# A new order for the first three chunks of a linear-attention and two-MoE kernel

## The chip, the cores and the metric

The program runs on one core of a Trainium2 chip. The metric is the device time in microseconds. Inputs and outputs are those of the reference, in float32.

## The reference, cut to what matters

```python
B, H, S, D = 4, 8, 768, 48
for t in range(S):                                   # linear attention with a decaying state
    cur = einsum('bhd,bhe->bhde', u * k_t, v_t)
    y_t = einsum('bhd,bhde->bhe', r_t, state + cur)
    state = w * state + einsum('bhd,bhe->bhde', k_t, v_t)
x = y.transpose(0, 2, 1, 3).reshape(3072, 384)
p = domain_probs / domain_probs.sum(-1)              # first MoE: 4 experts, all used, 1024 hidden
x = sum(p[:, e] * (relu(x @ w1[e]) @ w2[e]) for e in range(4))
# second MoE: 8 experts; each row goes to one expert by sorted gate logits, 384 rows each
out[rows of e] = relu(x[rows of e] @ v1[e]) @ v2[e]
```

## The kernel before, in words

The time axis is cut into 24 chunks of 128 positions, six to a batch element. A chunk's attention is done in closed form. Its transposed r and k (tile rkT, 512 KB) are multiplied by tables of powers of w (`mul`, L915). TensorE makes the scores (`scores`, L959), VectorE masks them (`am`, L965), and TensorE multiplies them with v and adds the part of the carried state S (`y_mm`, L983 and L987). The state for the next chunk comes from `state` (TensorE L1004, VectorE L1008, L1009 and L1011); it needs k times a table (`kn`, L929, on GpSimd). The diagonal term goes over GpSimd: `rk` (L921), `ru` (L925), then a sum on VectorE (`cc`, L940) and `cv` (L946). `x_add` (L994) joins both, and `tr` transposes x on TensorE (L1020) and stores it as an upper part by ScalarE (L1022) and a remainder by VectorE (L1023).

Every matrix of the MoE stages is held as two float32r parts, upper part and remainder, and a product is three matmuls: upper by upper, upper by remainder, remainder by upper (`up`, L1119, L1121, L1123; `down`, L1140, L1142, L1144). A weight of 384 KB comes into `raw` in pairs; ScalarE copies the upper part (L1058) and GpSimd or VectorE subtracts it (L1059), which is `split`.

The first MoE runs in 32 units of 384 rows by one expert. A unit is eight `up` blocks and three `down` groups. Its instruction stream has 48 ticks, one after every three matmuls, at which the Python program pops a step of a later chunk out of `queue` and puts it into the streams. Chunks 0, 1 and 2 are needed before the first unit, chunks 3, 4 and 5 before the second.

So there is a prologue. First come the tables of powers: `scan`, `inverse` and `mirror` for four pairs of heads, all on VectorE. Then a branch on a flag, and then chunks 0, 1 and 2 in an order written by hand, with bursts of empty matmuls (`warm`, L1284; also L703 and L724) between. All engines run their streams in the written order. Loads are issued by SyncE in the written order; a load waits there for its buffer.

Of the kernel before, what the change touches and what calls it, by code (L numbers as in the profile page):

```python
# [631 lines left out]
def rwkv_moe_moe(ctx, tc, A, out):  # L632
    nc = tc.nc
# [55 lines left out]
    with tc.tile_pool(name="psum0", bufs=1, space=bass.MemoryType.PSUM) as psum, tc.manual_schedule():  # L689
        v = nc.vector  # L690
        pb = psum.tile([128, 128], F32, name="pb")
        pf = psum.tile([1, 1], F32, name="pf")
        v.memset(busy, 0.0)
        v.memset(ones, 1.0)
        v.memset(zero, 0.0)
        v.memset(tp[:, 0, :, 64:65], 1.0)
        v.memset(tp[:, 1, :, 63:64], 1.0)
        v.memset(w128m, 0.0)
        make_identity(nc, ident)
        nc.gpsimd.iota(jp, pattern=[[1, 128]], base=0, channel_multiplier=-1)  # L700
# [20 lines left out]
        scan(0)  # L721
        v.tensor_scalar(flag, pf, 511.5, None, op0=OP.is_ge)
        for _ in range(36):
            nc.tensor.matmul(pb, busy.to_broadcast([128, 128]), busy.to_broadcast([128, 128]), start=True, stop=True)  # L724
        scan(1)
        inverse(0)
        scan(2)
        mirror(0)
        inverse(1)
        scan(3)  # L730
        mirror(1)
        inverse(2)
        inverse(3)
        mirror(2)
        mirror(3)
# [90 lines left out]
def main(ctx, tc, A, out, C, stepwise):  # L826
# [82 lines left out]
    def attn_steps(ck, detail=False):  # L909
# [6 lines left out]

        def rk():
# [23 lines left out]

        def cv():
# [3 lines left out]
            nc.gpsimd.tensor_tensor(r3, v3, st.pop((ck, "c")).to_broadcast([128, 8, 48]), op=OP.mult)  # L946

# [13 lines left out]
        def am(p0=0, p1=4):  # L961
            if p0 == 0:
                st[ck] = at.tile([128, 2, 4, 128], F32, name="am", bufs=1)
            for s in range(2):
# [11 lines left out]

        def y_mm():
            t, n = ld[ck]
            v = n[:, 384:768]
            y = psum.tile([128, D], F32, name="at", bufs=4)  # L980
            for p in range(4):
                if c:
                    nc.tensor.matmul(y[:, 96 * p:96 * p + 96], t[:, 0, p, :], S[ck - 1][:, p, :],  # L983
                                     start=True, stop=False)
                for s in range(2):
# [10 lines left out]

        def state():
            if c == 5:
                return
            t, n = ld[ck]  # L1000
            v = n[:, 384:768]
            p_ = psum.tile([128, 4, 96], F32, name="at", bufs=4)
            for p in range(4):
                nc.tensor.matmul(p_[:, p, :], n[:, 768 + 128 * p:896 + 128 * p], v[:, 96 * p:96 * p + 96],  # L1004
                                 start=True, stop=True)
            s = at.tile([128, 4, 96], F32, name="S", bufs=2)
            if c:
# [5 lines left out]

        def tr():
# [3 lines left out]
            p = psum.tile([128, 3, 128], F32, name="at", bufs=4)  # L1018
            for d in range(3):
                nc.tensor.transpose(p[:, d, :], x[:, 128 * d:128 * d + 128], ident)  # L1020
            cs = slice(128 * c, 128 * c + 128)
            nc.scalar.activation(XT[b][:, 0, :, cs], p, AF.Copy)  # L1022
            nc.vector.tensor_sub(XT[b][:, 1, :, cs], p, XT[b][:, 0, :, cs].bitcast(F32))  # L1023
            ld.pop(ck)

# [9 lines left out]
        if detail:  # L1035
            return dict(mul=mul, rk=rk, ru=ru, kn=kn, cc=cc, cv=cv, scores=scores, am=am, y=y_mm, x=x_add, state=state, tr=tr)
        return [lambda: (mul(nc.vector), pre()), pre2, nothing, att, nothing, yy, nothing, tr]
# [72 lines left out]
    def up(xT, c0, after1, before1, tick, tick1=lambda: None, place=None, H=None):  # L1110
        H = [] if H is None else H
        for f in range(FB):
            before1(f)
            p = psum.tile([128, D], F32, name="mm", bufs=4)
            w = W1[f]
            for k in range(3):
                ks = slice(128 * k, 128 * k + 128)
                xh, xl = xT[:, 0, k, c0:c0 + 384], xT[:, 1, k, c0:c0 + 384]
                nc.tensor.matmul(p, w[:, 0, ks], xh, start=(k == 0), stop=False)  # L1119
                tick1()  # L1120
                nc.tensor.matmul(p, w[:, 0, ks], xl, start=False, stop=False)  # L1121
                tick1()
                nc.tensor.matmul(p, w[:, 1, ks], xh, start=False, stop=(k == 2))  # L1123
                if k < 2:
                    tick()
# [103 lines left out]
    def tick():  # L1229
# [41 lines left out]
    else:  # L1271
        load_chunk(0)
        load_chunk(1)
        load_w(1, A["w1"], wl[0], 0)
        load_chunk(2)
        for q in range(1, 4):
            load_w(1, A["w1"], wl[0], q)
        consts_in()
        load_chunk(3)
        def warm(n):  # L1280
            p = psum.tile([128, 128], F32, name="mm", bufs=4)
            b = C["busy"].to_broadcast([128, 128])
            for _ in range(n):
                nc.tensor.matmul(p, b, b, start=True, stop=True)  # L1284

        def pkn_in():
            pt = psum.tile([128, 4, 128], F32, name="at", bufs=4)
            for p in range(4):
# [11 lines left out]
        a["mul"](nc.gpsimd, 0, 1)  # L1300
        a["mul"](nc.gpsimd, 1, 2)
        a["mul"](nc.vector, 2, 4)
        a["scores"](0, 1)
        warm(6)
        a["scores"](1, 2)
        pkn_in()
        a["am"](0, 2)
        a["scores"](2, 4)
        a["rk"]()
        a["ru"]()  # L1310
        a["am"](2, 4)
        a["kn"]()
        b["mul"](nc.vector)
        warm(8)
        a["cc"]()
        w128_in()
        b["rk"]()
        a["cv"]()
        a["y"]()
        a["state"]()  # L1320
        b["kn"]()
        b["scores"](0, 4)
        a["x"]()
# [6 lines left out]
        c["scores"](0, 4)  # L1330
        b["cc"]()
        b["cv"]()
        b["y"]()
        c["am"]()
        c["ru"]()
        split(1, 0, wl[0])
        b["x"]()
        c["cc"]()
        c["state"]()
        a["tr"]()  # L1340
        c["cv"]()
        split(1, 1, wl[0])
        split(1, 2, wl[0])
        split(1, 3, wl[0])
# [12 lines left out]
    nxt_chunk = [6]
    for ui, (i, blk) in enumerate(units):
# [353 lines left out]
```

## Time and profile before

| | us |
|---|---|
| median of 3 runs | 1229.07 (1228.4 to 1231.1) |
| profiled execution, its own time | 1224.69 |
| span of the profiled execution | 1222.9 |
| TensorE busy | 1199.3 (98%) |
| mean granted clock of TensorE | 0.988 of full |

The time of an execution is a little longer than the span from the first to the last instruction (here by 1.8 us). The granted clock is the share of full speed that TensorE was given: 1.00 is 2.4 GHz and 0.50 is 1.2 GHz. Busy time of an engine doesn't tell whether its clock was full. In the rows, PE is the matmul side of TensorE, PEld its weight load, DVE is VectorE, ACT ScalarE, POOL GpSimd and SPq the queue of SyncE, which issues the loads.

### The profile page before, as it was taken

To read this page: it belongs to the slowest core of one execution; us is meant where nothing else is said; L and a number is where in the kernel's file an instruction comes from. 1 tells how busy PE (TensorE), PEld (TensorE's weight loads), DVE (VectorE), ACT (ScalarE), POOL (GpSimd) and SP (SyncE) were. 2 spreads that over 40 slices of the span, in tenths; PEclk is the share of its full clock that TensorE was granted. 3 is DMA by queue.
4 is the path that set the end of the run, shared out by engine and by line. 5 is a ranking of instruction groups with operands and counts; after the bars stand their busy time and mean duration, and the time that the engine had idled before them with its cause. 6 is when DMAs were issued, how large, how long until landed. Compare 5 with 4: busy or idle time off the path is not lost. (4 is left out here: it accounts for less than half of the span.)

```text
span 1222.9 us, 20930 instructions
## 1 busy us (share of the span) xinstructions
PE 1199.3 (98%) x7842; PEld 1165.4 (95%) x7842; DVE 621.7 (51%) x1650; ACT 277.5 (23%) x590; POOL 354.7 (29%) x376
## 2 busy tenths in 40 slices
PE   8999999999999999999999999999999999999995
PEld 8999999999999999999999999999998888899995
DVE  6543333367333335863333368289665766663320
ACT  1322222222222222222222222223220111122221
POOL 6544343402333332243333323122200022122210
PEclk8899999999999999999999999999999999999998
DMA  6567555434887876578777745778620576667770
GB/s 259 198 242 271 201 193 195 143 123 137 259 275 245 281 245 245 181 243 284 248 274 250 236 152 191 251 269 311 239 103 21 181 289 219 212 228 272 280 285 26
DMA packets 95929, 267.64 MB, mean 219 GB/s; under 512 B 11328, under 2 KB 15552, under 8 KB 95680
## 3 DMA queue, kind: packets, MB, share of 16 engines
q1 hardware_dynamic: 92736, 256.67, 60.8%
q0 software_dynamic: 3072, 9.44, 2.1%
q8 instruction: 66, 1.08, 0.4%
q14 instruction: 55, 0.45, 0.1%
HBM read 181.13 MB, written 84.93 MB: 218 GB/s over the span
## 5 line engine op out<-in xcount | busy, mean ns | idle before, releaser
L1119 PE MATMUL mm<-xT,w 128*128 128x384 f32 x960 | 327.3, 341 | 1.2 <-ACT xT L1022 0.6
L1121 PE MATMUL mm<-xT,w 128*128 128x384 f32 x960 | 323.4, 337 | 0.3
L1123 PE MATMUL mm<-xT,w 128*128 128x384 f32 x960 | 322.6, 336 | 0.0
L1140 PE MATMUL mm<-w,h 128*128 128x384 f32 x939 | 317.1, 338 | 0.8 <-DMA w<-w2s 0.8
L1142 PE MATMUL mm<-w,h 128*128 128x384 f32 x939 | 315.5, 336 | 0.0
L1144 PE MATMUL mm<-w,h 128*128 128x384 f32 x939 | 315.2, 336 | 0.0
L1127 ACT ACTIVATE h<-mm 128x384 fp32r<-128x384 f32 x313 | 154.1, 492 | 617.6 <-PE mm L1123 572.1
L1128 DVE SCALAR_TENSOR_TENSOR h<-mm,h 128x384 fp32r<-128x384 f32 x313 | 173.8, 555 | 212.5 <-ACT h L1127 211.7
L1059 POOL TENSOR_TENSOR ws<-raw,ws 128x384 fp32r<-128x384 f32 x128 | 138.1, 1086 | 363.0 <-ACT ws L1058 332.5
L1119 PEld LDWEIGHTS mm<-xT,w 128*128 128x128 f32 x960 | 180.9, 188 | 4.5 <-ACT xT L1531 0.8
L1121 PEld LDWEIGHTS mm<-xT,w 128*128 128x128 f32 x960 | 180.8, 188 | 1.6 <-DVE xT L1532 0.8
L1123 PEld LDWEIGHTS mm<-xT,w 128*128 128x128 f32 x960 | 180.8, 188 | 0.1
L1140 PEld LDWEIGHTS mm<-w,h 128*128 128x128 f32 x939 | 176.3, 188 | 1.5 <-ACT ws L1058 1.1
L1142 PEld LDWEIGHTS mm<-w,h 128*128 128x128 f32 x939 | 176.3, 188 | 0.9 <-issue 0.4
L1144 PEld LDWEIGHTS mm<-w,h 128*128 128x128 f32 x939 | 176.3, 188 | 0.4
L1404 DVE SCALAR_TENSOR_TENSOR acc<-mm,dp,acc 128x384 f32<-128x384 f32 x72 | 44.4, 617 | 149.6 <-PE mm L1144 149.4
L1156 DVE SCALAR_TENSOR_TENSOR scr<-acc,wg 128x384 f32<-128x384 f32 x192 | 116.8, 645 | 0.1
L1059 POOL TENSOR_TENSOR w<-raw,w 128x384 fp32r<-128x384 f32 x60 | 60.8, 1028 | 115.6 <-ACT w L1058 115.6
L1058 ACT ACTIVATE ws<-raw 128x384 fp32r<-128x384 f32 x128 | 65.0, 522 | 111.2 <-DMA v2s<-ws 56.8
L1515 POOL DMA_INDIRECT acc<-x2d,idx x24 | 23.8, 990 | 150.1 <-DVE xl L504 109.5
L1651 POOL DMA_INDIRECT out_dram<-acc,idx x23 | 23.5, 1022 | 129.9 <-ACT acc L1649 94.2
L987 PE MATMUL at<-rkv,am 128*128 128x48 f32 x352 | 50.3, 272 | 0.0
(247 smaller groups left out, 937.1 us busy)
## 6 DMA issues: line engine op xcount, KB each, us to landing
w<-w1s SPq DMA_DIRECT2D x72, 384.0 KB, 4.2
w<-w2s SPq DMA_DIRECT2D x72, 384.0 KB, 6.3
raw<-in_v_dram SPq DMA_DIRECT2D x64, 384.0 KB, 4.1
v1s<-ws SPq DMA_DIRECT2D x64, 384.0 KB, 3.0
v2s<-ws SPq DMA_DIRECT2D x64, 384.0 KB, 3.0
w<-v1s SPq DMA_DIRECT2D x64, 384.0 KB, 6.7
w<-v2s SPq DMA_DIRECT2D x64, 384.0 KB, 5.9
rkv<-in_rkv_dram SPq DMA_DIRECT2D x22, 640.0 KB, 6.3
```

Of the source, the lines that this page charges most:

```text
L987: nc.tensor.matmul(y[:, 48 * h:48 * h + 48], st[ck][:, s, p, :], v[:, 48 * h:48 * h + 48], start=not c, stop=bool(s) or not c)
L1058: nc.scalar.activation(w[:, 0], r, AF.Copy)
L1059: engine.tensor_tensor(w[:, 1], r, w[:, 0].bitcast(F32), op=OP.subtract)
L1119: nc.tensor.matmul(p, w[:, 0, ks], xh, start=(k == 0), stop=False)
L1121: nc.tensor.matmul(p, w[:, 0, ks], xl, start=False, stop=False)
L1123: nc.tensor.matmul(p, w[:, 1, ks], xh, start=False, stop=(k == 2))
L1127: nc.scalar.activation(h[:, 0], p, AF.Relu)
L1128: nc.vector.scalar_tensor_tensor(h[:, 1], p, 0.0, h[:, 0].bitcast(F32), op0=OP.max, op1=OP.subtract)
L1140: nc.tensor.matmul(p, h[:, 0, ts], w[:, 0], start=(f == 0), stop=False)
L1142: nc.tensor.matmul(p, h[:, 0, ts], w[:, 1], start=False, stop=False)
L1144: nc.tensor.matmul(p, h[:, 1, ts], w[:, 0], start=False, stop=(f == FB - 1))
L1156: nc.vector.scalar_tensor_tensor(scr[e % 2], x, 1.0, wg[:, e], op0=OP.mult, op1=OP.mult, accum_out=to[:, e:e + 1])
```

## The change

The tables: the eight copies of `mirror` go from VectorE to ScalarE, whose table load is moved ahead of them by a one-element copy; `scan(1)` is put ahead of the flag. The two copies that fill `w128m` go to ScalarE too.

The loads: weight pair 0 is issued ahead of chunk 1, and pair 1 ahead of chunk 2; pairs 2 and 3 follow chunk 2.

The three chunks: `mul`, `scores`, `am` and `y` are cut into halves and put in a new order. `mul` of chunk 1 and of chunk 2 is shared between GpSimd (one half) and VectorE (the other), where VectorE did it whole before. `ru` of chunk 0 and `cv` of chunks 0 and 2 go from GpSimd to VectorE. Chunk 1 gets a buffer of its own for the masked scores. The state of chunk 2 (`kn`, `st`, `S`) goes behind the transposes: `kn` behind the split of weight block 4 on GpSimd, the matmuls into the first tick of unit 0. All eight splits of the first weights stand ahead of unit 0 (before, four of them stood inside it, on VectorE). There are 48 warming matmuls after the branch in place of 38.

Unit 0: the steps of chunks 3, 4 and 5 are interleaved by a written list of 24 steps, and pairs of steps are popped until 8 are left (before: 11). From the step `head` (which has `mul`) to the step `att` (which has `scores`) of chunk 4 there are nine ticks; before there were four.

In every unit, block 0 of `up` does the six matmuls with the upper part of x first and the three with its remainder last.

```diff
         def mirror(p):
-            v.tensor_copy(tp[:, 1, p, 0:63], rev(tp[:, 0, p, 65:128]))
-            v.tensor_copy(tp[:, 0, p, 0:64], rev(tp[:, 1, p, 64:128]))
+            nc.scalar.activation(tp[:, 1, p, 0:63], rev(tp[:, 0, p, 65:128]), AF.Copy)
+            nc.scalar.activation(tp[:, 0, p, 0:64], rev(tp[:, 1, p, 64:128]), AF.Copy)
...
+            order = [(a, b, k) for k in range(3) for a, b in ((0, 0), (0, 1), (1, 0))]
+            if f == 0:
+                order.sort(key=lambda o: o[1])
+            for n, (a, b, k) in enumerate(order):
+                nc.tensor.matmul(p, w[:, a, 128 * k:128 * k + 128], xT[:, b, k, c0:c0 + 384], start=(n == 0), stop=(n == 8))
...
-        if n == 1 and len(queue) > (11 if ticks[0] < 48 else 12):
+        if n == 1 and len(queue) > (8 if ticks[0] < 48 else 12):
...
         load_chunk(0)
+        load_w(1, A["w1"], wl[0], 0)
         load_chunk(1)
-        load_w(1, A["w1"], wl[0], 0)
+        load_w(1, A["w1"], wl[0], 1)
         load_chunk(2)
...
-                nc.vector.tensor_copy(w128m[r, :, 48 * s:48 * s + 48], w128[r].to_broadcast([48, 4, 48]))
+                nc.scalar.activation(w128m[r, :, 48 * s:48 * s + 48], w128[r].to_broadcast([48, 4, 48]), AF.Copy)
...
+        a["am"](0, 2)
+        a["kn"]()
+        a["am"](2, 4)
+        warm(8)
+        a["y"](0, 2)
+        a["ru"](V)
+        a["y"](2, 4)
+        b["mul"](G, 0, 2)
+        a["cc"]()
+        a["st"]("mm")
+        b["mul"](V, 2, 4)
+        b["rk"]()
+        a["cv"](V)
+        b["scores"](0, 2)
+        b["scores"](2, 4)
+        a["S"]()
+        b["kn"]()
+        b["am"](0, 2)
+        b["am"](2, 4)
+        warm(16)
+        b["y"](0, 2)
+        b["ru"]()
+        c["mul"](V, 0, 2)
+        c["mul"](G, 2, 4)
+        b["st"]("mm")
+        a["x"]()
+        b["cc"]()
+        c["scores"](0, 2)
+        c["rk"]()
+        b["S"]()
+        c["scores"](2, 4)
+        b["y"](2, 4)
+        c["am"](0, 2)
+        b["cv"]()
+        a["tr"]("m")
+        c["am"](2, 4)
+        c["ru"]()
+        c["y"](0, 2)
+        b["x"]()
+        w1(0, G)
+        c["y"](2, 4)
+        c["cc"]()
+        c["cv"](V)
+        b["tr"]("m")
+        a["tr"]("c")
+        c["x"]()
+        w1(1, G)
+        warm(12)
+        c["tr"]("m")
+        b["tr"]("c")
+        w1(2, G)
+        c["tr"]("c")
+        warm(12)
+        w1(3, V)
+        w1(4, G)
+        w1(5, V)
         c["kn"]()
-        b["ru"]()
...
+        w1(6, G)
+        w1(7, V)
+        queue.append(lambda: (c["st"](), c["S"]()))
+        s = {ck: attn_steps(ck) for ck in (3, 4, 5)}
+        load_chunk(4)
+        s[3]["head"]()
+        nothing = lambda: None
+        queue.extend([
+            s[3]["pre2"], nothing, s[3]["att"], lambda: load_chunk(5), s[4]["head"], s[3]["yy"], nothing,
+            s[4]["pre2"], s[3]["tr"], nothing, s[4]["att"], nothing, s[5]["head"], s[4]["yy"], nothing,
+            s[5]["pre2"], lambda: (s[4]["tr"](), load_chunk(6)), nothing, s[5]["att"], nothing, s[5]["yy"], nothing, s[5]["tr"]])
```

## Rows read from the trace of the kernel before

**Rows 1.** Prologue: start:end us, busy by engine; then granted clock, DMA share, GB/s

```profile
0.00:35.30 35.30, 32.04 (x247) 29.97 (x248) 22.79 (x56) 5.11 (x9) 23.89 (x28) 0.76 0.72 261
```

**Rows 2.** Timeline of TensorE: first matmul of unit 0, first two of unit 1

```profile
35.31 0.47 PE L1119 MATMUL mm<-xT,w 128*128 128x384 f32 x1
...
79.56 0.45 PE L1119 MATMUL mm<-xT,w 128*128 128x384 f32 x1 [0.58 <-ACT xT L1022]
80.15 0.45 PE L1121 MATMUL mm<-xT,w 128*128 128x384 f32 x1
```

**Rows 3.** Three stretches of the prologue and one of unit 0, columns as rows 1

```profile
14.00:16.00 2.00, 0.85 (x11) 0.69 (x8) 1.90 (x4) 0.00 (x0) 0.78 (x2) 1.00 1.03 400
...
18.00:20.00 2.00, 2.00 (x17) 1.78 (x14) 1.52 (x3) 0.00 (x0) 2.00 (x2) 0.59 1.02 412
...
32.00:34.00 2.00, 2.00 (x17) 1.88 (x16) 0.91 (x2) 0.61 (x2) 1.88 (x2) 0.50 0.65 232
...
52.20:56.00 3.80, 3.80 (x15) 3.73 (x13) 2.29 (x5) 0.91 (x2) 3.26 (x4) 0.55 0.00 0
```

**Rows 4.** Timeline of VectorE and GpSimd: two-input work side by side

```profile
5.41 1.32 POOL L915 TENSOR_TENSOR rkT<-rkT,tp 128x256 f32<-128x256 f32 x2 [3.88 <-DVE tp L711]
...
10.43 1.24 DVE L915 TENSOR_TENSOR rkT<-rkT,tp 128x1024 f32<-128x1024 f32 x1
10.69 1.84 POOL L921 TENSOR_TENSOR rkv<-rkv 128x384 f32<-128x384 f32 x1
...
12.58 2.09 DVE L1297 COPY w128m<-w 48x192 f32<-48x192 f32 x2
...
13.28 1.27 POOL L929 TENSOR_TENSOR rkv<-rkv,pkn 128x512 f32<-128x512 f32 x1
```

**Rows 5.** Groups of the prologue by form: busy us, mean ns of one, idle before

```profile
L929 POOL TENSOR_TENSOR xT<-xT,pkn 128x512 f32<-128x512 f32 x2 | 2.5, 1270 | 0.1
L925 POOL TENSOR_TENSOR xT<-xT,u_b 128x384 f32<-128x384 f32 x2 | 2.0, 998 | 0.1
L946 POOL TENSOR_TENSOR rkv<-rkv,cc 128x384 f32<-128x384 f32 x2 | 1.6, 825 | 0.7 <-DVE cc L940 0.7
L1059 POOL TENSOR_TENSOR w<-raw,w 128x384 fp32r<-128x384 f32 x4 | 3.9, 1000 | 0.3 <-ACT w L1058 0.3
L915 DVE TENSOR_TENSOR xT<-xT,tp 128x1024 f32<-128x1024 f32 x2 | 2.4, 1216 | 0.0
L1022 ACT ACTIVATE xT<-at 128x384 fp32r<-128x384 f32 x3 | 1.5, 491 | 19.5 <-PE at L1020 19.5
L1290 ACT ACTIVATE pkn<-at 128x512 f32<-128x512 f32 x1 | 0.6, 597 | 2.7 <-PE at L1289 2.7
```

**Rows 6.** Timeline of TensorE: steps at full clock, and `y` (20.23 on) at half

```profile
20.23 0.71 PE L983 MATMUL at<-S,rkT 128*128 128x96 f32 x2
...
21.51 0.71 PE L983 MATMUL at<-S,rkT 128*128 128x96 f32 x2
...
45.92 0.52 PE L1020 MATMUL at<-ident,x 128*128 128x128 f32 x3 [0.21 <-DVE x L994]
...
51.18 1.16 PE L959 MATMUL at<-rkT 48*128 48x128 f32 x16 [1.59 <-DVE rkT L915]
...
57.15 0.43 PE L983 MATMUL at<-S,rkT 128*128 128x96 f32 x2
...
57.82 0.43 PE L983 MATMUL at<-S,rkT 128*128 128x96 f32 x2
...
59.16 1.10 PE L1004 MATMUL at<-rkv 128*128 128x96 f32 x8
```

**Rows 7.** Timeline of unit 0: a split on VectorE, the last split on GpSimd

```profile
38.21 0.55 DVE L1059 TENSOR_TENSOR w<-raw,w 128x384 fp32r<-128x384 f32 x1
...
62.87 1.01 POOL L1059 TENSOR_TENSOR w<-raw,w 128x384 fp32r<-128x384 f32 x1 [4.14 <-ACT w L1058]
```

**Rows 8.** DMA issues of 6.6 to 6.8 us: KB each, us from issue to landing

```profile
xT<-in_rkv_dram SPq DMA_DIRECT2D x1, 640.0 KB, 9.0
```

More of the change, by code (lines that the diff above doesn't have):

```diff
@@ L724, in rwkv_moe_moe @@
             nc.tensor.matmul(pb, busy.to_broadcast([128, 128]), busy.to_broadcast([128, 128]), start=True, stop=True)
-        scan(1)
         inverse(0)
-        scan(2)
         mirror(0)
         inverse(1)
+        mirror(1)
+        scan(2)
+        inverse(2)
+        mirror(2)
         scan(3)
-        mirror(1)
-        inverse(2)
         inverse(3)
-        mirror(2)
         mirror(3)
@@ L962, in am @@
             if p0 == 0:
-                st[ck] = at.tile([128, 2, 4, 128], F32, name="am", bufs=1)
+                if detail and ck == 1:
+                    st[ck] = wg.rearrange("p e d -> p (e d)")[:, 0:1024].rearrange("p (a b c) -> p a b c", a=2, b=4)
+                else:
+                    st[ck] = at.tile([128, 2, 4, 128], F32, name="am", bufs=1)
             for s in range(2):
@@ L975, in yy, with y_mm @@
             x_add()
-        def y_mm():
+        def y_mm(p0=0, p1=4):
             t, n = ld[ck]
             v = n[:, 384:768]
-            y = psum.tile([128, D], F32, name="at", bufs=4)
-            for p in range(4):
+            if p0 == 0:
+                st[ck, "y"] = psum.tile([128, D], F32, name="mm" if detail else "at", bufs=4)
+            y = st[ck, "y"]
+            for p in range(p0, p1):
                 if c:
@@ L1012, in state, with tr, tr_mm @@
             S[ck] = s
-        def tr():
+        def state():
+            if c < 5:
+                state_mm()
+                state_new()
+        def tr(parts="mc"):
+            if "m" in parts:
+                tr_mm()
+            if "c" in parts:
+                tr_out()
+        def tr_mm():
             x = st.pop(ck)
@@ L1023, in tr @@
             nc.vector.tensor_sub(XT[b][:, 1, :, cs], p, XT[b][:, 0, :, cs].bitcast(F32))
-            ld.pop(ck)
+            if not detail:
+                ld.pop(ck)
         def fetch():
@@ L1035, in attn_steps @@
         if detail:
-            return dict(mul=mul, rk=rk, ru=ru, kn=kn, cc=cc, cv=cv, scores=scores, am=am, y=y_mm, x=x_add, state=state, tr=tr)
+            return dict(mul=mul, rk=rk, ru=ru, kn=kn, cc=cc, cv=cv, scores=scores, am=am, y=y_mm, x=x_add, st=state_mm, S=state_new, tr=tr)
+        if ck < 6:
+            return dict(head=lambda: (mul(nc.vector), pre()), pre2=pre2, att=att, yy=yy, tr=tr)
         return [lambda: (mul(nc.vector), pre()), pre2, nothing, att, nothing, yy, nothing, tr]
@@ L1115, in up @@
             w = W1[f]
[L1116 to L1124, printed above, removed]
+            order = [(a, b, k) for k in range(3) for a, b in ((0, 0), (0, 1), (1, 0))]
[3 more added lines that the diff above has]
+                nc.tensor.matmul(p, w[:, a, 128 * k:128 * k + 128], xT[:, b, k, c0:c0 + 384], start=(n == 0), stop=(n == 8))
+                if n % 3 < 2:
+                    tick1()
+                elif n < 8:
                     tick()
@@ L1272, in main @@
         load_chunk(0)
+        load_w(1, A["w1"], wl[0], 0)
         load_chunk(1)
-        load_w(1, A["w1"], wl[0], 0)
+        load_w(1, A["w1"], wl[0], 1)
         load_chunk(2)
-        for q in range(1, 4):
-            load_w(1, A["w1"], wl[0], q)
+        load_w(1, A["w1"], wl[0], 2)
+        load_w(1, A["w1"], wl[0], 3)
         consts_in()
@@ L1303, in main @@
+        a["mul"](G, 0, 1)
+        a["mul"](G, 1, 2)
         a["scores"](0, 1)
-        warm(6)
+        a["mul"](V, 2, 4)
+        a["rk"]()
+        pkn_in()
         a["scores"](1, 2)
-        pkn_in()
+        w128_in()
+        a["scores"](2, 4)
         a["am"](0, 2)
-        a["scores"](2, 4)
-        a["rk"]()
-        a["ru"]()
+        a["kn"]()
         a["am"](2, 4)
-        a["kn"]()
-        b["mul"](nc.vector)
         warm(8)
+        a["y"](0, 2)
+        a["ru"](V)
+        a["y"](2, 4)
@@ L1323, in main @@
         a["x"]()
-        c["mul"](nc.vector)
-        b["am"]()
-        b["state"]()
+        b["cc"]()
+        c["scores"](0, 2)
         c["rk"]()
-        c["kn"]()
-        b["ru"]()
[L1330 to L1344, printed above, removed]
@@ L1356, in main @@
+    if stepwise:
+        for ck in (3, 4, 5):
+            enqueue(ck)
     units = [(i, blk) for i in range(16) for blk in range(2)]
@@ L1380, in after1 @@
             if ui == 0 and not stepwise:
-                if f < 4:
-                    split(1, f + 4, wl[0], nc.vector)
-                elif f == 5:
+                if f == 5:
                     late_consts()
```

54 lines of the change are left out of this document (22 added, 32 removed).

## The prediction

> **What bounds the kernel now.** I read the page first: TensorE is busy for 98% of the span. Then I cut the span into stretches. In the prologue the mean granted clock is only 0.76, and VectorE and GpSimd are each busy for two thirds of it [rows 1]. The edits lie in the prologue and in unit 0, so I took the timeline of TensorE there: unit 0 starts at 35.31 us and unit 1 at 79.56 us [rows 2]. Much can be won only there; behind them the instruction stream stays the same but for block 0 of each `up`.
>
> Short stretches show what goes wrong. Between 14 and 16 us TensorE works for 0.85 us of 2.00; between 18 and 20 us the clock averages 0.59, and it is still at half (1.2 GHz) between 32 and 34 us [rows 3]. At half clock a pair of heads in `y` takes 1.28 us (20.23 to 21.51), at full clock 0.67 us (57.15 to 57.82) [rows 6]. So the second half of the prologue is matmuls at half speed, and ahead of it stands a wait for VectorE and GpSimd.
>
> That wait comes from two engines that exclude each other. VectorE's `mul` runs from 10.43 to 11.67; GpSimd's `rk`, issued at 10.69, takes 1.84 us and ends at 12.53, about 0.9 us after `mul`. The two copies into `w128m` took 2.09 us, until 14.67, just behind the end of GpSimd's `kn` at 14.55 [rows 4]. The reader is to see that an instruction on GpSimd and one on VectorE with two SBUF inputs (or a copy from SBUF to SBUF) add up instead of overlapping. The Trainium skill (Advanced Engine Details and Errata, Mode Summary) says that VectorE's second SBUF port is shared with GpSimd, and that the two block each other. By that rule, the trace agrees.
>
> **Entry into unit 0.** With that exclusion, GpSimd's work and VectorE's two-input instructions are one sum. It begins at 5.41, where GpSimd starts its two halves of `mul`, 1.32 us [rows 4]; I leave that start, since chunk 0 is loaded as before.
>
> GpSimd, up to the split of block 0: the `mul` of chunk 0 at 1.32, three `rk` at about 1.0, two `kn` at 1.27, two halves of `mul` (128x512, so 1.27 like `kn`), two `ru` at 1.0, b.cv at 0.83, a split at 1.0: 13.2 us. VectorE's share: three halves of `mul` at 0.61, the product of b's state, a.ru, a.cv and c.cv [rows 5]. `ru` and `cv` on VectorE are not in the trace; the nearest row is its 128x384 split at 0.55 [rows 7], the upper bound is GpSimd's own 1.0. I take 0.5 each, as neighbours overlap a little; with the state's product that is 2.0, and 3.8 in all. 5.41 + 13.2 + 3.8 = 22.4 us for the end of c.cv. A remainder of `tr` and c.x, 0.55 each, bring 23.5.
>
> TensorE must agree. Of that sum 8.1 us lie ahead of the end of a.cv, at 13.5; a's state (0.5) and the first half of b's masked scores (0.75) end at 14.8. From 15.0 TensorE has b.y 2.7, `state` 0.95, c's scores 1.1, a transpose 0.45 and c.y 2.7 at full clock [rows 6]: 22.9. Then come a transpose (0.45), 12 warming matmuls (0.8), c's transpose when c.x is there (0.45), and ScalarE's copy of 0.49 [rows 5] beside the last 12 (0.8): unit 0 starts at 25.4, which is 9.9 us less than 35.31. The bounds: 24.4, if the warming bursts hide, and 32.4, if the clock falls at 18.4 as before, since about 7 us of matmuls then take twice as long.
>
> **Tables and loads, costed at nothing.** `mirror` on ScalarE is not in the trace. Its copies of 128x384 and 128x512 take 0.49 and 0.60 [rows 5], so by that slope 64 columns take 0.22; between 0 and 0.49 each, eight of them, interleaved with the reciprocals, end near 6.4 us. What hides them is GpSimd's `mul`, which runs until 6.73. Without that cover it would be at most 2 us. The Trainium skill has a rule against this (ScalarE: Activation LUTs, Rules for kernel authors): plain arithmetic belongs on VectorE, up to about three times faster per element in bf16. By that rule these copies would cost a little more than before; no run here shows it.
>
> Weight pair 0 now goes ahead of chunk 1, and pair 1 ahead of chunk 2. 384 KB at some 400 GB/s [rows 3] are about 1 us; chunk 1 lands that much later, near 9.8, and GpSimd is done with a.kn at 9.5. The rest of chunk 2 landed 9.0 us after its issue near 6.7 [rows 8], while three weight pairs shared the time; now one stands ahead and two behind. I expect 16 to 17 us, and its `rk` comes at 17.7 in the sum. If that cover goes, each us late is a us.
>
> **A new wait: `st` of chunk 2.** It stands in tick 1, behind three matmuls of unit 0, so at about 26.0. It needs c.kn, which stands on GpSimd behind the splits of blocks 1, 2 and 4. Those follow ScalarE's copies, and these stand between its copies of x: block 1 ends at 23.5, block 2 at 25.4; ScalarE copies c's x until 25.15, then blocks 3 and 4 until 26.05; the split of block 4 ends at 27.2, VectorE's of block 5 takes its turn until 27.7, `kn` ends at 28.7 (between 28.4 and 29.0, by whose turn comes first). All of unit 0 on TensorE is queued behind `st`, so it idles for 2.7 us. The bounds are 0, if GpSimd gets ahead, and 3. Before, a wait ahead of `scores` in unit 0 (1.76 us idle, 1.59 of it put down to `mul`) [rows 6] was followed by 3.8 us at a mean clock of 0.55 [rows 3]: 3.8 x 0.45 = 1.7 us lost. I take the same loss once here.
>
> **Unit 0 and later.** It lasted 79.56 - 35.31 = 44.25 us [rows 2]. Off go the 1.76 us of idling, as nine ticks now stand between chunk 4's `mul` and its scores in place of four; the 1.7 us of cold clock; and 0.2 us of waiting for x [rows 6]. On come `st` with 0.9, the wait of 2.7 and its cold clock of 1.7: 45.9, so 1.65 longer. At unit 1 the upper parts now hide the remainder that is waited for between 79.56 and 80.15, about 0.4 us [rows 2]. The second MoE's first block may win as much; I take 0.
>
> **Sum:** -9.9 + 1.65 - 0.4 = -8.65 us against the profiled 1224.69: 1216.0. The median of the three runs stands 4.4 us above that execution, so I forecast 1229.07 - 8.65 = 1220.4.
>
> **Rivals.** *GpSimd gets ahead.* If c.kn is done before 26, the wait and its cold clock don't appear: 4.4 us better, 1216.0, and with unit 0 at 24.4, 1215.0. For it speaks that these weights lie in SBUF by then; against it that GpSimd has the longest sum. 20%.
>
> *The clock falls in the prologue.* From 18 to 34 us TensorE was busy and the clock stayed at half [rows 3]; the new order has no warming burst between 14 and 23 us either. Then unit 0 starts between 28 and 32.4, and the wait at `st` is gone, since c.kn doesn't depend on TensorE's clock. Unit 0 is then 2.8 us shorter than before: -7.3 - 2.8 - 0.4 to -2.9 - 2.8 - 0.4, 1218.6 to 1223.0. 23%.
>
> *The gain is given back.* The reorder doesn't shorten the chain, because the shared `mul` costs 1.27 + 0.61 where VectorE alone took 1.22, twice, and late loads stretch the rest: within 0.2% of before. 7%.
>
> *Slower.* GpSimd now has eight splits of `w2` between three heads in unit 0; by the sum of its work the last one is done near 54.5, and `down` needs it near 55. Before, it ended at 63.9 [rows 7]. Each us beyond 55 is one on TensorE. It decides once the turns on the shared port add 9 us, from about 64; at 70 it gives 1235. 5%.
>
> **How the numbers follow.** The forecast has 45%. The range takes in the bounds: 1215.0 (no wait at `st`) to 1225.0 (clock down at 18 us and 2 us of waits for `w2`). A measurement of this kernel can't tell less than 0.2% (2.5 us) from no change. Faster: 45 + 20 + 23 = 88%; same 7%; slower 5%.
>
> **What would show it.** Unit 0's first matmul near 25.4, with a clock of 1.00 from 15 to 25 us; an idle TensorE behind its third matmul, ended by `kn` on GpSimd near 28.7; no wait ahead of chunk 4's scores; no `mirror` on the path. A clock of 0.50 before 25 us, or a first matmul after 30, makes me wrong, and so does a `down` of unit 0 that waits for GpSimd.

## The result, and the profile after

Four runs of the changed kernel have a median of **1219.1 us** (1218.26 to 1219.53), four runs of the kernel before 1229.37 us (1228.4 to 1231.1). The ratio is 0.9914, with a 95% interval of 0.9897 to 0.9931: the change takes 0.9% off. The forecast was 1220.4, faster.

The profiled execution took 1219.4 us, its span 1217.6. The timeline of TensorE of the kernel after (start, duration, engine, line, operation, count, idle time before and what ended it), at the places of [rows 2] and [rows 6], with a burst of warming matmuls ahead of them and one row of GpSimd behind them:

```profile
14.06 1.11 PE L1313 MATMUL at<-busy 128*128 128x128 bf16 x16
...
25.59 0.79 PE L1149 MATMUL mm<-xT,w 128*128 128x384 f32 x3
29.04 1.37 PE L1011 MATMUL at<-xT 128*128 128x96 f32 x8 [2.66 <-POOL xT L931]
...
72.37 6.53 PE L1149 MATMUL mm<-xT,w 128*128 128x384 f32 x36 [0.58 <-ACT xT L1047]
...
27.41 1.57 POOL L931 TENSOR_TENSOR xT<-xT,pkn 128x512 f32<-128x512 f32 x1
```

Unit 0 starts 9.72 us earlier than in [rows 2], and then an idle TensorE waits 2.66 us for `kn` on GpSimd (L931), which ends at 28.98: the wait that the prediction put behind the third matmul. Unit 1 starts 7.19 us earlier. Its first block now runs without the gap of [rows 2] between first and second matmul.

The stretches of [rows 3] that mattered, and those around the new wait, of the kernel after (busy time of PE, PEld, DVE, ACT and POOL, then granted clock, DMA share, GB/s):

```profile
0.00:25.50 25.50, 23.88 (x249) 22.06 (x249) 20.66 (x49) 7.18 (x20) 17.17 (x22) 1.00 0.85 309
...
14.00:16.00 2.00, 1.75 (x24) 1.49 (x20) 2.00 (x5) 0.00 (x0) 2.00 (x3) 1.00 1.00 400
...
18.00:20.00 2.00, 2.00 (x25) 1.84 (x24) 1.97 (x5) 0.00 (x0) 1.85 (x3) 1.00 1.03 416
...
28.00:30.00 2.00, 0.96 (x8) 0.96 (x8) 2.00 (x2) 0.00 (x0) 2.00 (x2) 0.95 0.98 356
30.00:32.00 2.00, 2.00 (x8) 2.00 (x8) 1.97 (x3) 0.00 (x0) 2.00 (x2) 0.50 1.02 380
32.00:34.00 2.00, 2.00 (x10) 2.00 (x9) 1.66 (x3) 0.90 (x2) 1.92 (x3) 0.70 1.01 353
```

The prologue's clock is 1.00 where it was 0.76 [rows 1], and TensorE works for 1.75 us between 14 and 16 where it worked for 0.85 [rows 3]; 16 of its 24 matmuls there are the warming burst at 14.06. Behind the new wait the clock is at half between 30 and 32 us: 2 x 0.05 + 2 x 0.50 + 2 x 0.30 = 1.7 us lost.

The timelines of ScalarE, GpSimd and VectorE of the kernel after, at the work of [rows 4] and at the end of the forecast's sum:

```profile
6.15 0.26 ACT L719 ACTIVATE tp<-tp 128x64 f32<-128x64 f32 x1 [0.33 <-DVE tp L715]
...
8.57 0.72 ACT L1326 ACTIVATE w128m<-w 48x192 f32<-48x192 f32 x2
...
8.82 1.27 POOL L931 TENSOR_TENSOR rkv<-rkv,pkn 128x512 f32<-128x512 f32 x1 [0.69 <-ACT pkn L1319]
...
11.81 1.00 POOL L923 TENSOR_TENSOR rkv<-rkv 128x384 f32<-128x384 f32 x1 [0.55 <-DMA rkv<-in_rkv_dram]
...
13.28 1.62 DVE L948 TENSOR_TENSOR rkv<-rkv,cc 128x384 f32<-128x384 f32 x1
...
21.98 0.56 DVE L948 TENSOR_TENSOR xT<-xT,cc 128x384 f32<-128x384 f32 x1
```

The two copies into `w128m` take 0.72 us on ScalarE, where VectorE took 2.09 [rows 4]. The last `mirror` ends at 6.41. The same `cv` takes 1.62 us on VectorE beside GpSimd's `kn`, and 0.56 at 21.98; it ends at 22.54, where the sum said 22.4. The last split of unit 0's `w2` ends at 56.67 (63.88 before [rows 7]), and no `down` of unit 0 waits for it.

### The profile page after: what moved, and what is told of

It reads as the page before. It is cut to its first block, busy times and chain, and to the rows that moved or that the text cites. A ratio compares the mean times of both kernels' runs of the same rounds, so it can differ in the third digit from the quotient of the medians.

```text
span 1217.6 us, 20969 instructions
## 1 busy us (share of the span) xinstructions
PE 1191.8 (98%) x7852; PEld 1158.5 (95%) x7852; DVE 625.5 (51%) x1646; ACT 279.6 (23%) x601; POOL 356.2 (29%) x376
## 5 line engine op out<-in xcount | busy, mean ns | idle before, releaser
L1149 PE MATMUL mm<-xT,w 128*128 128x384 f32 x2880 | 529.6, 338 | 1.2 <-ACT xT L1047 0.6
L1149 PEld LDWEIGHTS mm<-xT,w 128*128 128x128 f32 x2880 | 498.6, 188 | 5.1 <-ACT xT L1047 0.8
L1087 POOL TENSOR_TENSOR ws<-raw,ws 128x384 fp32r<-128x384 f32 x128 | 135.6, 1067 | 365.3 <-ACT ws L1086 323.9
L1087 POOL TENSOR_TENSOR w<-raw,w 128x384 fp32r<-128x384 f32 x61 | 65.7, 1089 | 112.1 <-ACT w L1086 112.0
L1456 DVE TENSOR_SCALAR acc<-mm,dp 128x384 f32<-128x384 f32 x24 | 14.8, 617 | 60.8 <-PE mm L1172 60.8
L995 PE MATMUL at<-rkv,am 128*128 128x48 f32 x320 | 44.7, 266 | 0.4 <-DVE am L971 0.4
L995 PEld LDWEIGHTS at<-rkv,am 128*128 128x128 f32 x320 | 41.7, 192 | 0.7 <-DVE am L971 0.7
L1184 DVE SCALAR_TENSOR_TENSOR scr<-w2r,wg 128x384 f32<-128x384 f32 x64 | 41.1, 684 | 0.0
L948 POOL TENSOR_TENSOR rkv<-rkv,cc 128x384 f32<-128x384 f32 x21 | 17.4, 829 | 78.2 <-DVE cc L942 77.6
```

The costliest lines, as they stand in the source:

```text
L995: nc.tensor.matmul(y[:, 48 * h:48 * h + 48], st[ck][:, s, p, :], v[:, 48 * h:48 * h + 48], start=not c, stop=bool(s) or not c)
L1087: engine.tensor_tensor(w[:, 1], r, w[:, 0].bitcast(F32), op=OP.subtract)
L1149: nc.tensor.matmul(p, w[:, a, 128 * k:128 * k + 128], xT[:, b, k, c0:c0 + 384], start=(n == 0), stop=(n == 8))
L1184: nc.vector.scalar_tensor_tensor(scr[e % 2], x, 1.0, wg[:, e], op0=OP.mult, op1=OP.mult, accum_out=to[:, e:e + 1])
```

## The experiments

Each start of unit 0 and unit 1 below is that of the first matmul, from the timeline of TensorE. "At unit 1" is the start of unit 1 against 79.56 of [rows 2]. Where only one execution was timed, its total is given, but the verdict rests on the trace up to unit 1: totals of one kernel differ by more than most of these edits.

**The kernel before, once more**, with no edit. The medians differ by 10.3 us, but the two traces by only 5.3 (spans 1222.9 and 1217.6).

> The kernel before, unchanged, in one more profiled execution. Its runs had a median 4.7 us above its first profiled execution (1224.69), and the two traces at hand differ by 7.6 us in the first MoE but by 5.3 us at the end. If the second MoE varies from one execution to the next (theory), the first 800 us repeat within 0.3 us (unit 0 at 35.3, unit 1 at 79.6) and the end comes 2 to 6 us later than 1222.9. If it is the prologue that varies (rival), unit 1 itself starts later than 80.5 us.

It took 1228.87 us, 4.2 more than the execution of the prediction's trace. Its windows, same columns:

```profile
8.00:10.00 2.00, 0.55 (x5) 0.31 (x4) 1.90 (x4) 0.60 (x1) 1.51 (x2) 1.00 0.94 349
10.00:12.00 2.00, 2.00 (x21) 1.84 (x21) 1.41 (x4) 0.00 (x0) 1.51 (x2) 0.93 1.01 401
12.00:14.00 2.00, 2.00 (x11) 2.00 (x11) 1.97 (x4) 0.52 (x1) 0.38 (x2) 0.50 1.02 421
```

TensorE idled early (0.55 us of work between 8 and 10), and the clock was at half from 12 us on, not from 18 as in [rows 3]. The timelines of VectorE and TensorE of this run show what came ahead of it:

```profile
6.72 0.92 DVE L718 COPY tp<-tp 128x63 f32<-128x63 f32 x1
...
7.77 0.99 DVE L719 COPY tp<-tp 128x64 f32<-128x64 f32 x1
...
8.85 0.69 DVE L915 TENSOR_TENSOR rkT<-rkT,tp 128x512 f32<-128x512 f32 x1
...
9.93 1.04 PE L959 MATMUL at<-rkT 48*128 48x128 f32 x8 [1.46 <-DVE am L965]
```

and the same `mul` in the trace of [rows 2]:

```profile
7.29 1.20 DVE L915 TENSOR_TENSOR rkT<-rkT,tp 128x512 f32<-128x512 f32 x1 [0.20 <-DVE tp L719]
```

Two copies of `mirror` took 0.92 and 0.99 us, the other six 0.16 to 0.18. They end at 7.64 and 8.76, each just behind an instruction of GpSimd (`rk` at 7.59, `ru` at 8.70). So `mul` of chunk 0 came 1.6 us later than in the trace of [rows 2], and TensorE waited 1.46 us for the masks behind it, where it waited 0.49. In this execution `mirror` itself lay on the path. That this wait made the clock fall is likely and not shown.

Unit 0 started at 38.73, unit 1 at 83.07: 3.5 us later than in [rows 2], and of the 4.1 us between the spans that is nearly all. So it is the prologue that varies, by where the clock falls. Against this execution the changed kernel is 10.7 us ahead at unit 1 (83.07 - 72.37), which is what the medians show.

**`state` of chunk 2 later**, from tick 1 to tick 7:

```diff
-        queue.append(lambda: (c["st"](), c["S"]()))
+        queue.append(lambda: None)
...
-  s[3]["pre2"], nothing, s[3]["att"], lambda: load_chunk(5), s[4]["head"],
+  s[3]["pre2"], nothing, s[3]["att"], lambda: (load_chunk(5), c["st"](), c["S"]()), s[4]["head"],
```

> The changed kernel with the state of chunk 2 (matmuls and VectorE) moved from tick 1 to tick 7. Theory of the prediction taken alone: the wait of 2.7 us behind the third matmul goes and the cold clock of 1.6 us with it, so unit 1 starts 4.3 us earlier, near 68.1. Rival, read from the trace after: the scores of chunk 3 at tick 6 need its `mul` on VectorE, which ends at 31.3, and would now be asked for at 28.7; then 2.6 us of the wait come back there and unit 1 starts near 72.

The waits of TensorE up to 200 us (engine and line, what it waited for, us in total, times, longest):

```profile
PE at L961 <- DVE xT L917: 2.5, 1, 2.5
...
PE at L991 <- DVE S L1020: 0.9, 1, 0.9
```

The wait at `st` is gone, and another of 2.5 us stands two steps on, at chunk 3's scores (31.81 us), which need VectorE's `mul`; then 0.9 for the new S. The clock stayed at 1.00 between 26 and 36 us. Unit 1 started at 71.97, only 0.4 us earlier. The wait at `st` was one place where TensorE meets a backlog of VectorE and GpSimd; moving it alone shows the next place. The run took 1216.73 us.

**`state` and chunk 3's scores later** (ticks 4 and 6 of a new list):

```diff
-        queue.append(lambda: (c["st"](), c["S"]()))
...
+            nothing, s[3]["pre2"], nothing, lambda: (c["st"](), c["S"]()), lambda: load_chunk(5), s[3]["att"],
+            s[4]["head"], nothing, s[3]["yy"], s[4]["pre2"], s[3]["tr"], s[4]["att"], nothing, s[5]["head"], s[4]["yy"], nothing,
```

> The changed kernel with the state of chunk 2 at tick 6, the scores of chunk 3 at tick 9, its `yy` at tick 13, and the list kept at 24 steps. If VectorE's and GpSimd's backlog is what is waited for, both waits shrink to under 0.6 us in all, the clock stays at 1.00 between 26 and 36 us, and unit 1 starts 3.5 to 4.3 us earlier than after the change (72.4), near 68.5. If the backlog only moves on (rival), a wait of over 1.5 us shows at a later step of unit 0 and unit 1 starts after 71.

Left are three waits for masked scores of chunk 3 and later, 1.0 us in all, and 0.7 us for S. The clock stayed at 1.00 from 26 to 46 us, also around these waits:

```profile
34.00:36.00 2.00, 1.35 (x8) 1.03 (x7) 1.97 (x4) 0.90 (x2) 2.00 (x3) 1.00 0.93 336
```

Unit 0 started at 25.57, unit 1 at 70.42, 1.95 us earlier than after. 1215.41 us. The direction is as expected, the size about half, since those waits came in.

**`mul` whole on VectorE**, in place of the two shared halves:

```diff
-        b["mul"](G, 0, 2)
...
-        b["mul"](V, 2, 4)
+        b["mul"](V)
...
-        c["mul"](V, 0, 2)
-        c["mul"](G, 2, 4)
+        c["mul"](V)
```

> The changed kernel with `mul` of chunks 1 and 2 whole on VectorE again. Theory (the two engines exclude each other, so the shared form costs 1.27 + 0.61 us in place of 1.22): the sum of work shrinks by 1.3 us, and the split of block 0 on GpSimd and the start of unit 0 come 0.5 to 1.3 us earlier (20.5 and 25.6 now). Rival (the halves overlap): both come 0.5 to 1.2 us later.

Unit 0 started at 24.67, 0.92 us earlier: the shared halves cost about that. (The last experiment below has this form too; its unit 0 started at 24.94.) The wait at `st` stayed:

```profile
28.12 1.13 PE L1011 MATMUL at<-xT 128*128 128x96 f32 x8 [2.65 <-POOL xT L931]
```

but the clock did not fall behind it (windows of this run):

```profile
28.00:30.00 2.00, 1.88 (x14) 1.88 (x15) 2.00 (x2) 0.00 (x0) 2.00 (x3) 1.00 0.89 285
30.00:32.00 2.00, 2.00 (x13) 1.75 (x14) 1.97 (x4) 0.98 (x3) 1.92 (x2) 1.00 1.01 363
```

So unit 1 came at 69.39, 3.0 us earlier than after: 0.9 at the entry, 1.7 that the clock did not take, and 0.4 more (the two waits for masked scores near 50 us, 0.20 and 0.17 in the kernel after, are gone). The run took 1213.2 us. A wait of the same length cost the clock in one program's execution and not in the other's. What decides that is not shown.

**The upper parts of x not first** (the `sort` of block 0's nine matmuls taken out):

> The changed kernel with the nine matmuls of block 0 of `up` in the order of before. Theory: at unit 1 the second matmul waits again for VectorE's remainder, 0.4 us, so everything behind it comes 0.4 us later; at unit 0 the same wait appears, but the wait at the state of chunk 2 takes it in. Rival (ScalarE's upper part is what is waited for): no difference at unit 1.

```profile
72.17 6.95 PE L1147 MATMUL mm<-xT,w 128*128 128x384 f32 x36 [0.58 <-ACT xT L1047]
```

A wait of 0.15 us for the remainder (VectorE, L1048) came back at unit 0, behind its first matmul; the wait at `st`, 2.24 us here, is shorter by as much as these matmuls are longer. At unit 1 no such wait is listed, but the first 36 matmuls take 6.95 us where they take 6.53 after. At the first of them this run is 7.4 us ahead of [rows 2] (72.17 against 79.56), and the same 36 matmuls later; the whole change goes from 7.2 to 7.6 there. So the size agrees with the 0.4 us of the prediction. 1217.63 us, one execution, whose total could not tell it.

**No warming bursts in the new order** (bursts of 16, 12 and 12 empty matmuls taken out):

> The changed kernel without the burst of 16 warming matmuls ahead of b.y and without both of 12 at the end of the prologue; it leaves out no other work. If the order alone keeps TensorE busy enough, the clock stays at 1.00 from 14 to 25 us and unit 0 starts up to 1 us earlier than at 25.6 (theory: the gain is the order). If the bursts are what holds the clock (rival), it falls to 0.50 between 14 and 22 us, and unit 0 starts between 27 and 32 us.

```profile
12.00:14.00 2.00, 1.33 (x19) 1.04 (x18) 2.00 (x4) 0.00 (x0) 1.92 (x2) 1.00 1.01 412
14.00:16.00 2.00, 2.00 (x14) 1.93 (x15) 1.89 (x5) 0.00 (x0) 2.00 (x3) 0.90 1.01 404
16.00:18.00 2.00, 2.00 (x12) 1.83 (x12) 1.45 (x4) 0.00 (x0) 2.00 (x2) 0.50 1.05 389
```

The clock fell shortly before 16 us and unit 0 started at 30.04, 4.45 us later than with the bursts; unit 1 at 78.04, 1224.9 us. The bursts are part of what holds the clock in the new order, and of the three it is the first: the two of 12 stand behind the fall (from 23.81 us on in the kernel after). This is also the second rival of the prediction made real, and 30.04 lies in its 28 to 32.4. But that rival said that the wait at `st` goes when the clock falls, and it stayed:

```profile
33.49 2.02 PE L1011 MATMUL at<-xT 128*128 128x96 f32 x8 [2.12 <-POOL xT L931]
```

`kn` came later too (31.86, not 27.41): it stands on GpSimd behind splits, one of which waited 4.66 us for ScalarE, and ScalarE had waited 4.75 us for the transposes on TensorE. Unit 0 lasted 48.0 us, longer than before and not 2.8 us shorter.

**Bursts alone in the kernel before**:

```diff
         b["scores"](0, 4)
+        warm(24)
...
         b["state"]()
+        warm(16)
```

> The kernel before with two more bursts of warming matmuls, 24 behind b's scores and 16 behind b's state, which fill the time in which TensorE waited. If the half clock is what made the prologue long (theory: about 7 of its 9.7 us), the clock stays at 1.00 and unit 0 starts near 28 to 29 us in place of 35.3 (38.8 in the second execution). If the order of the work on VectorE and GpSimd is what made it long (rival), unit 0 starts after 33 whatever the clock.

The clock stayed at 1.00 from 8 to 36 us; unit 0 started at 30.32, 5.0 us earlier than in [rows 2] and between the two theories. The wait at the scores of unit 0 stayed (1.6 us), the clock was at half behind it, and 4.6 us were left at unit 1. 1224.03 us. So a held clock is worth 5.0 us at the entry against that execution, and 8.4 against the one repeated above (38.73 - 30.32); the chain under it is as long as before. The second is the nearer comparison: here, as in the repeated run, two copies of `mirror` took 0.92 and 0.98 us and `mul` of chunk 0 began at 8.96.

**Tables on ScalarE alone in the kernel before** (the eight copies of `mirror` and the two into `w128m`, with the one-element copy that moves ScalarE's table load ahead of them; nothing else):

```diff
-            v.tensor_copy(tp[:, 1, p, 0:63], rev(tp[:, 0, p, 65:128]))
-            v.tensor_copy(tp[:, 0, p, 0:64], rev(tp[:, 1, p, 64:128]))
+            nc.scalar.activation(tp[:, 1, p, 0:63], rev(tp[:, 0, p, 65:128]), AF.Copy)
+            nc.scalar.activation(tp[:, 0, p, 0:64], rev(tp[:, 1, p, 64:128]), AF.Copy)
+
+        nc.scalar.activation(C["scr1"][0:1, 0:1], ones[0:1], AF.Copy)
...
-                nc.vector.tensor_copy(w128m[r, :, 48 * s:48 * s + 48], w128[r].to_broadcast([48, 4, 48]))
+                nc.scalar.activation(w128m[r, :, 48 * s:48 * s + 48], w128[r].to_broadcast([48, 4, 48]), AF.Copy)
```

> The kernel before with only the copies of the tables (`mirror` and the two into `w128m`) on ScalarE. Theory: VectorE's 2.09 us behind GpSimd go, a's state is ready 1.5 to 2 us earlier than at 15.3, b's matmuls follow, and unit 0 starts 2 to 7 us earlier than in the kernel before, the more the later the clock falls. Rival (the copies were hidden): a's state comes within 0.4 us of 15.3 and unit 0 between 35 and 39.

Timelines of this run, at the state of chunk 0, at unit 0 and at unit 1:

```profile
12.32 0.73 ACT L1299 ACTIVATE w128m<-w 48x192 f32<-48x192 f32 x2 [3.34 <-DVE w L1296]
13.08 0.56 DVE L1013 TENSOR_TENSOR S<-at,w128m 128x384 f32<-128x384 f32 x1 [0.80 <-ACT w128m L1299]
...
26.32 0.42 PE L1121 MATMUL mm<-xT,w 128*128 128x384 f32 x1
...
69.95 0.44 PE L1121 MATMUL mm<-xT,w 128*128 128x384 f32 x1 [0.58 <-ACT xT L1024]
```

The state of chunk 0 is multiplied at 13.08, 1.7 us earlier than in the kernel before (14.78 there, 0.1 us behind the end of the copies [rows 4]). The clock holds, unit 0 starts at 26.32: 9.0 us of the whole change's 9.7 come with ten copies in this execution. How much of it is `mirror` and how much the copies into `w128m` was not run apart. At unit 1 this kernel is 9.6 us ahead of [rows 2], more than the whole change with 7.2. 1215.57 us. The same kernel, timed five times:

> The kernel before with only the copies of the tables on ScalarE, now timed. In one execution it was 1215.57 us, and unit 1 came 9.6 us earlier than before, against 7.6 us in the changed kernel. If that holds over executions (theory: the two engines' turns and with them the clock, not the new order, made most of the gain), its median is 1214 to 1218 and its ratio to before at most that of the changed kernel (0.9914). If its clock is as unsteady as that of the kernel before (rival), which fell at 18 us in one execution and near 12 us in another, the median is above 1219 and the runs differ by over 3 us.

Five runs, median 1215.87 us (1215.69 to 1221.21), against 1227.13 for eleven of the kernel before; ratio 0.9908 (0.9895 to 0.9921). Four of the five lie within 1.1 us at a mean clock of 0.995 to 0.996. So the median is the theory's, though the runs differ by 5.5 us, as the rival has it. The fifth, at 1221.21, was the profiled one, with 0.990:

```profile
14.00:16.00 2.00, 1.17 (x9) 1.00 (x9) 1.36 (x3) 0.00 (x0) 0.21 (x1) 1.00 1.03 410
...
18.00:20.00 2.00, 2.00 (x12) 2.00 (x12) 1.11 (x2) 0.00 (x0) 1.95 (x2) 0.53 1.01 409
...
28.00:30.00 2.00, 2.00 (x11) 2.00 (x11) 0.00 (x0) 0.00 (x0) 1.92 (x3) 0.50 0.77 201
```

In it the clock fell at 18 us, though the same program had held it in the run before, and unit 0 started at 32.79. Its timelines show a difference ahead of the fall:

```profile
14.69 1.23 DVE L917 TENSOR_TENSOR xT<-xT,tp 128x1024 f32<-128x1024 f32 x1 [0.64 <-DMA xT<-in_rkT_dram]
...
15.96 1.75 PE L961 MATMUL at<-xT 48*128 48x128 f32 x16 [0.56 <-DVE xT L917]
```

VectorE waited 0.64 us for the load of chunk 2, and so chunk 2's scores came behind 0.56 us of idling; in the run before, both began without a wait (`mul` at 14.02, scores at 15.42). So the load's landing is a likely cause of the two courses, and not a shown one. Both courses of one program stand here side by side: 32.79 - 26.32 = 6.5 us is the price of the clock at the entry (with the 0.5 us of that load), and 35.31 - 32.79 = 2.5 us is what the copies give when the clock falls all the same.

**The old order of loads in the new kernel** (chunk 1 ahead of weight pair 0, chunk 2 ahead of pair 1):

> The changed kernel with the loads in the order of before (weight pair 0 behind chunk 1, pairs 1 to 3 behind chunk 2). By the prediction the loads were hidden: unit 0 starts within 0.3 us of 25.6. Rival: the new order costs, since GpSimd idles 0.55 us for the second half of chunk 1; then unit 0 starts 0.4 to 0.9 us earlier.

Unit 0 started at 25.16 and unit 1 at 71.93, both 0.4 us earlier than after; the wait at `st` (2.7 us) and the half clock behind it were the same. 1216.74 us. The loads are worth nothing on the path. Whether the new order costs 0.4 is not shown: four executions of one and the same prologue (the kernel after, both kernels with a later `state`, and the one without the upper parts first) started unit 0 between 25.36 and 25.86.

**Tables, the list of steps and upper parts first, in the kernel before**, with the three chunks, their splits and the loads in their old order (pairs of steps are popped until 8 are left, as in the whole change):

```diff
+            order = [(a, b, k) for k in range(3) for a, b in ((0, 0), (0, 1), (1, 0))]
+            if f == 0:
+                order.sort(key=lambda o: o[1])
...
+        s = {ck: attn_steps(ck) for ck in (3, 4, 5)}
...
+            nothing, s[3][1], nothing, s[3][3], lambda: load_chunk(5), s[4][0], s[3][5], nothing,
+            s[4][1], s[3][7], nothing, s[4][3], nothing, s[5][0], s[4][5], nothing,
```

> The kernel before with three parts of the change: the tables on ScalarE, the list of steps in unit 0 (without the state of chunk 2, which stays in the prologue), and the upper parts first. The prologue keeps its old order, loads and splits. Theory: to the 9.6 us of the tables come the 1.76 us of idling ahead of chunk 4's scores and 0.4 us at unit 1, so unit 1 starts 11 to 12 us earlier than before, near 68.2, and the median is 1213 to 1216. Rival (the list brings its own wait, as it did in the changed kernel at the state and the scores): unit 1 no earlier than 69.5.

Six runs, median **1213.52 us** (1211.73 to 1220.07); ratio 0.9897 (0.9877 to 0.9917). Waits of TensorE up to 200 us, and the starts of the two units:

```profile
PE at L1006 <- POOL rkv L931: 0.7, 1, 0.7
...
PE at L989 <- DVE am L967: 0.2, 1, 0.2
```

```profile
26.70 3.38 PE L1122 MATMUL mm<-xT,w 128*128 128x384 f32 x18
...
67.87 6.51 PE L1122 MATMUL mm<-xT,w 128*128 128x384 f32 x36 [0.58 <-ACT xT L1024]
```

Inside unit 0 only 0.18 us of waiting is left (for masked scores, at 45.69), and it lasts 41.2 us, where it lasted 44.25 before and 46.8 after. The rest of the change (chunks in halves, splits, loads, `state` moved) saves 1.1 us at the entry (25.59 against 26.70), and unit 0 gives back 5.6: 4.4 of it are the wait at `st` and the half clock behind it (2.66 + 1.7), and 0.9 the matmuls of `st`; neither is in unit 0 here, since chunk 2's state stands ahead of it. Against the whole change this run's trace is 4.5 us ahead at unit 1. The intervals of the two ratios (0.9877 to 0.9917 and 0.9897 to 0.9931) overlap, and the two were not timed side by side, so that this version beats the whole change is likely and not shown by the times.

**The whole change, `mul` whole, `state` and chunk 3's scores later**:

> The changed kernel with `mul` of chunks 1 and 2 whole on VectorE, and with the state of chunk 2 at tick 6 and the scores of chunk 3 at tick 9. By the parts, entry 0.9 us earlier and 2 to 2.7 us less waiting in unit 0: unit 1 near 68.5 to 69, median 1212.5 to 1215.5. If the backlog of VectorE and GpSimd sets the pace of unit 0 (rival), the later steps take the 0.9 us back and unit 1 starts near 70.

Six runs, median 1217.73 us (1213.17 to 1221.62), ratio 0.9922 (0.9901 to 0.9943), at mean clocks of 0.990 to 0.997: no gain over the whole change that these runs can tell. In the profiled one unit 0 started at 24.94 and there is no wait at `st`, but three small ones together (0.65 us for S, 0.60 and 0.18 for masked scores, between 34.5 and 36.9 us) left TensorE idle for half of a stretch, and the clock fell behind them (it stayed at half for two more stretches, up to 44 us):

```profile
34.00:36.00 2.00, 1.01 (x6) 0.52 (x4) 1.97 (x4) 0.90 (x2) 2.00 (x3) 1.00 0.97 369
36.00:38.00 2.00, 1.56 (x10) 1.44 (x10) 2.00 (x4) 0.00 (x0) 2.00 (x2) 0.85 1.03 413
38.00:40.00 2.00, 2.00 (x11) 2.00 (x11) 0.50 (x2) 0.00 (x0) 1.92 (x3) 0.50 1.03 415
```

Unit 1 came at 72.52, no earlier than after. The half clock took 3.4 us between 36 and 46; without it unit 1 would have come near 69.1, as expected. The kernel with `state` and scores later had the same three waits, 0.65, 0.60 and 0.18 us, and its clock stayed at 1.00. So the repairs are shown to take away waits, but not to keep the clock, and over six runs they gain nothing that can be told.

## Why the prediction was right, point by point

**The entry** was forecast at 25.4 and came at 25.59. The end of c.cv was forecast at 22.4 and came at 22.54. The sum hit with parts that were off. The end of a.cv was forecast at 13.5 and came at 14.90. GpSimd stood idle for 0.69 us (for ScalarE's `pkn`) and 0.55 us (for chunk 1's load, which landed near 11.8 and not near 9.8), which the sum did not hold, so the two engines must have overlapped later on by about that much more than it allowed; this is worked out from the sum, not seen in a row. The exclusion of the two engines, on which it rests, shows in the `cv` of 1.62 and 0.56 us. So the number is confirmed, and the mechanism too, each part of it only roughly; that the parts offset to 0.2 us is luck.

**Tables, costed at nothing.** The cost was right: the last copy ended at 6.41 (6.4 forecast). But the prediction wrote the 9.9 us down to the new order as a whole, and did not price what the ten copies give by leaving VectorE. The runs show that they alone bring 9.0 of the 9.7 us when the clock holds: 2.5 by the shorter chain, 6.5 by the clock. And in the repeated run of the kernel before, `mirror` on VectorE did lie on the path, with copies of up to 0.99 us and 1.46 us of waiting on TensorE; the prediction's one trace (no copy above 0.44) doesn't show that. The rule that was weighed there, that plain arithmetic belongs on VectorE (the Trainium skill, ScalarE: Activation LUTs, Rules for kernel authors), agrees with the durations: the copy at L719 took 0.26 us on ScalarE and 0.18 on VectorE. It decides wrongly here all the same, because on VectorE such a copy also stands in turn with GpSimd (2.09 us for two), and on ScalarE it doesn't (0.72).

**The clock in the prologue** held, as the forecast had it, in the four runs of the changed kernel, as far as their mean clocks of 0.994 and 0.995 tell; only one has a trace. In six more traces, of kernels with the new order and its bursts, it held up to unit 0 as well. It does not hold by itself: without the bursts it fell, and in the kernel with the tables alone it held in one trace and fell in the next. The rival that gave this 23% was real, and it was argued from a misreading: that no warming burst stands between 14 and 23 us. The burst of 16 stands at 14.06, where TensorE would have idled, and the prediction's sum for TensorE doesn't count it. The forecast named the right course of the clock without naming what held it. Of the rival, the time of unit 0 came true in the run without bursts, and the claim that the wait at `st` then goes did not (2.12 us).

**The new wait** was forecast at 2.7 us, ended by `kn` at 28.7, with 1.7 us lost to the clock. Measured: 2.66 us, 28.98, 1.7 us. What the prediction did not see is that this wait hides another: with `state` moved, chunk 3's scores wait 2.5 us.

**Unit 0** was forecast at 45.9 us and lasted 46.78; 0.4 of the 0.9 us between are two waits for masked scores near 50 us, 0.2 each. No wait stands ahead of chunk 4's scores, as forecast. The 0.4 us at unit 1 came.

**The sum.** Forecast against the prediction's own trace: -8.65 us. Measured there: -7.6 just behind unit 1's start, and -5.3 at the end of the span. The last 2.3 us went in the second MoE, where the waits of TensorE from 800 us on are longer than in the kernel before. First the kernel after, then the kernel before:

```profile
PE at L1583 <- DMA acc<-x2d,idx: 2.2, 2, 1.5
PE at L471 <- DVE oh L448: 1.3, 2, 1.0
PE mm L1168 <- DMA w<-w2s: 1.2, 1, 1.2
PE at L502 <- issue: 0.9, 1, 0.9
```

```profile
PE at L1529 <- DMA acc<-x2d,idx: 1.6, 2, 1.1
PE mm L1140 <- DMA w<-w2s: 0.8, 1, 0.8
...
PE at L471 <- DVE oh L448: 0.3, 1, 0.3
```

0.6, 1.0, 0.4 and 0.9 us are 2.9. The traces of the tables alone (9.6 us ahead at unit 1, 9.2 at the end) and of the old loads (7.6 and 8.0) don't lose this. Neither does the kernel with `mul` whole, whose program is the changed one from the end of the prologue on (10.2 and 11.6): its wait for `oh` is 0.3 us and it has none of L502's 0.9. So the changed code by itself doesn't bring the loss; from unit 1 to the end such kernels take 1141.9 to 1145.2 us, the kernel after the longest of them. In the medians the loss is not seen, because the prediction's trace of before was itself 4.4 us below the median. The step "minus 8.65 against the profiled execution, plus 4.4 to the median" treated these 4.4 us as lying around the change; the repeated run shows that 3.5 of them lie inside the prologue, where the clock falls at 18 or at 12 us, and where the change takes them away. So that 1220.4 stood 1.3 us from the result is owed to two errors that offset: too much gain against that trace, and too little gain against a common execution.

**The rivals.** GpSimd did not get ahead. The `mul` that is shared does cost, as its rival said, 0.9 us in place of 1.3 (twice 1.27 + 0.61 against 1.22), but it does not eat the gain. The splits of `w2` ended 7 us earlier than before and held nothing up.

## What to carry to other kernels

When VectorE and GpSimd stand in turn, look first for small instructions on VectorE that a third engine can do, even one that is slower at them: ten copies brought nearly the whole entry here in the runs whose clock held. The new order with its bursts held the clock up to unit 0 in seven traces of seven; the ten copies with the old order in two of three. Price a wait of TensorE with the half clock that may follow it, and expect it at the next meeting with the same backlog when it is moved. Where the time hangs on where a clock falls, profile the kernel before twice: here the second trace showed a cost of `mirror` that the first did not have.

## What the runs showed of the hardware

The same program ran with the clock falling at 18 us in one execution and at 12 us in another (unit 0 at 35.31 and 38.73), and the kernel with the tables alone held it in one and lost it at 18 us in the next (26.32 and 32.79); ahead of the early fall stood a wait of TensorE of 1.46 us, and ahead of that at 18 us in the tables' kernel two of 0.65 and 0.56. The two traces of the tables' kernel are from different chips; but of five runs of it on one chip four had a mean clock of 0.995 or more and one 0.990. Once it had fallen at 18 us there, TensorE was busy for all of the time until 30 us and the clock stayed at 0.50 to 0.53. Two waits of 2.66 and 2.65 us at the same instruction were followed by a half clock in one kernel and by a full one in the other; three smaller ones (0.65, 0.60 and 0.18 us), too, by a half clock in one kernel and by a full one in another. A copy of 128x64 on VectorE took 0.18 us in most places and 0.99 where GpSimd's `ru` ran beside it. Two copies of 48x192 took 2.09 us on VectorE beside GpSimd and 0.72 on ScalarE.
